# Folding half of batch 1's first DFT stage in a fused global filter and ReGLU FFN kernel

## The chip, the core and the metric

The kernel runs on one core of a Trainium2 chip. Its engines are TensorE (PE in the profile; its weight loads are PEld), VectorE (DVE), ScalarE (ACT), GpSimd (POOL) and SyncE (SP, which only issues DMAs here). The metric is the device time of one execution in microseconds (us). The kernel before was timed three times: 866.41, 866.97 and 868.27 us, median 866.97 us.

## The reference

```
def _attn_ref(x, filt_r, filt_i):            # x: (8, 3008, 256) float32
    X = np.fft.rfft(x, axis=1)
    Y = X * (filt_r + 1j * filt_i)[None, :, :]
    y = np.fft.irfft(Y, n=x.shape[1], axis=1)
    return y.astype(np.float32)

def _moe_ref(x, w_gate, w_val, w_out):       # x: (24064, 256); w: 256x1536, 256x1536, 1536x256
    gate = np.maximum(x @ w_gate, 0.0)
    val = x @ w_val
    return (gate * val @ w_out).astype(np.float32)
```

The second function takes the first one's output with batch and sequence flattened to 24064 tokens.

## The kernel before

**The DFT.** A sequence of 3008 is cut as 94 x 32 (n1, n2). Stage A is a real DFT of length 94 over n1, as a matrix product. Its result is turned so that n2 lies along the partitions, and stage B, the helper `fwd(b, i)`, does the length 32 part for one of six groups of frequencies. `product` multiplies by the filter, `add` joins the products, `inv` goes back along the 32, `load_d` fetches the result turned, and `item_c(k, h)` does the way back along the 94 for one block of 512 tokens, giving `yT`, the input of the FFN.

**Stage A in three forms.** Batch 0: `a_0` with the matrix `WA` (float32), an ACT copy into `AS0`, and a VectorE transpose in four quarters (`turn_0`). Batch 1, all in the prologue: sixteen items of `a_1`, each a 128x512 float32 product in two instructions. Items of the first half of d are copied to `AS1[0]` (a part of `dCb`) and go to DRAM and back (`store_half`, `load_half`); items of the second half go to two `asb` tiles and are transposed on VectorE (`turn_1`, one of four before the FFN, three at its steps 1, 7 and 12). Batches 2 to 7: `load_chunk` brings x in folded order, row n1 beside its mirrored row, `fold_chunk` makes sums and differences on GpSimd (six instructions per chunk, four chunks per batch), and `tiled_a` does 32 small matmuls into four PSUM banks, four copies (two ACT, two VectorE) into an `asb` tile and four stores to `Abuf`; later `load_at_tiled` reads `Abuf` back as `at`, with n2 along the partitions. Each of these stores and reads goes by the SP queue.

**The FFN.** 47 blocks of 512 tokens, twelve steps each. A step is `gv`: two matmuls for the value and two for the gate (128x512 each), an ACT copy `vsb`, and one VectorE instruction `prod` that does the relu and the product. Behind it `o_part` adds four 128x256 output matmuls for the block before; in block 0 there is no block before, so steps 0 to 11 have none. Everything else is hung on steps by a table written out by hand: `at_step(s, f)` calls f after `gv` and `o_part` of step s. All engines work in the order in which the code is written.

**Batch 1's due times.** `end` is 51 for batch 1 and its first two groups start at `end - 37`:

```
        end = (b * S // W - 1) * NFT + C_AT[0] - 5
        starts, gap = ((-37, -25, -13), 4) if b == 1 else ((-43, -30, -17), 5)
```

So `fwd(1, 0)` and `fwd(1, 1)` stand at step 14. They read all of batch 1's `at`.

**Banks.** The eight PSUM banks are handed out in the order in which the code frees them (`free.pop(0)`, `free.append`). A taker waits on the chip until the former owner's last reader is done.

**The prologue's order.** Stage A of batch 0, then `first_b`: for batch 0 `fwd`, products on VectorE and, for three of the twelve (i, e), on GpSimd by way of an ACT copy `xs`, and three inverse blocks `inv(0, q)`, with single items of batch 1 between them (`item(n)`). Then `turn_d` transposes batch 0's result on VectorE in two halves, seven items run beside it, `item_c(0, .)` makes the first `yT`, three more items, and the FFN starts. `warm(n)` issues n matmuls on constant data whose results nobody reads.

Of the kernel before, what the change touches and what calls it, by code (L numbers as in the profile page):

```python
# [116 lines left out]
def kernel(  # L117
# [44 lines left out]
    Abuf = [dram.tile([NROW * N2, D if b > 1 else D // 2], BF16, name=f"Abuf{b}") if b else None for b in range(B)]  # L162
# [9 lines left out]
    AS1 = [dCb[:, 32:48, :].rearrange("p n d -> p (n d)").rearrange("p (l c d) -> p l c d", l=NC2, d=D // 2)]  # L172
# [21 lines left out]
    WHOLE = ((0, 0, NX2 * D), (1, 0, NX2 * D))  # L194
# [3 lines left out]
    conj32 = pro.tile([128, 2], FP32, tag="conj32", bufs=1)  # L198
# [21 lines left out]
    def place_own():  # L220

        o = own.rearrange("p (k r g n) -> p k r g n", k=2, r=2, g=2)
        for i, t in enumerate((I2t, I2u)):
            nc.gpsimd.tensor_copy(t[96:, :, NG // 2 - 2:, :], o[:, i])
# [34 lines left out]

    def a_bank(n2, nn, d0, nd):  # L260

        psA = bank("psA", nn, nd)
        xf = XF[n2 // NX2].rearrange("p (n d) -> p n d", d=D)
        n = n2 % NX2
        nc.tensor.matmul(psA, WA, xf[:, n:n + nn, d0:d0 + nd], start=True, stop=True)  # L265
        return psA

    def a_0(n2, nn, d0, nd):

        psA = a_bank(n2, nn, d0, nd)  # L270
        dq = D // 4
        l, q = n2 % NC2, slice(d0 // dq, (d0 + nd) // dq)
        c = n2 // NC2
        dst = AS0.rearrange("p q (l c) e (g f) -> p l c g q e f", c=2, g=2)[:, l:l + nn, c // 2, c % 2]
        src = psA.rearrange("p n (q e f) -> p n q e f", e=dq // 2, f=2)
        for i in range(nd // dq):
            nc.scalar.copy(dst[:, :, q.start + i], src[:, :, i])
        done(psA)

    def a_1(p, s, h):  # L280

        psA = a_bank(NC2 * p + 4 * s, 4, h * D // 2, D // 2)
        if h and len(AS1) == 1:
            for _ in range(2):
                t = sb.tile([128, NC2 * D], BF16, tag="asb", bufs=3, name="asb")
                AS1.append(t.rearrange("p (l c d) -> p l c d", l=NC2, c=N2 // NC2))
        ts = AS1[1:] if h else AS1[:1]
        w = D // 2 // len(ts)
        for i, t in enumerate(ts):
            nc.scalar.copy(t[:, 4 * s:4 * s + 4, p, :], psA[:, :, i * w:(i + 1) * w])  # L290
        done(psA)

    def turn_a(dst, src):

        nc.vector.transpose(dst.bitcast(FP32).rearrange("p k d -> p d k"),
                            src.bitcast(FP32).rearrange("p n d -> p d n"))
# [6 lines left out]
    def turn_0(q):  # L303
        w = D // 8
        turn_pairs(ats[0][:, :, q * w:q * w + w], AS0[:, q])

    def turn_1(i):
        w = D // 8
        src = AS1[1 + i // 2].rearrange("p l c d -> p (l c) d")
        turn_a(ats[1][:, 1, :, i * w:i * w + w], src[:, :, i % 2 * w:i % 2 * w + w])  # L310

    def new_at(b):
        shape = [2, 32, D // 2] if b else [16, D // 2, 4]
        ats[b] = sb.tile([128, *shape], BF16, tag="at", bufs=1, name="at")

    def turn_d(h):

        e = slice(h * D // 4, h * D // 4 + D // 4)
        turn_pairs(D0[:, :, e], DS0[:, :, e])

    def store_half(b):
        w = N2 * D // 2
        for q in range(4):
            nc.sync.dma_start(_ap(Abuf[b], q * NG * w, [[w, NG], [1, w]]),
                              AS1[0][32 * q:32 * q + NG].rearrange("p l c d -> p (l c d)"))

    def load_half(b):
        w = N2 * D // 2
        for q in range(4):
            nc.sync.dma_start(ats[b][32 * q:32 * q + 32, 0, 0:NG, :],  # L330
                              _ap(Abuf[b], q * NG * w, [[D // 2, 32], [w, NG], [1, D // 2]]))
# [16 lines left out]
    def fold_chunk(b, j):  # L348

        xp = XP[j]  # L350
        t = fs.tile([128, 2, 512], FP32, tag="fold", bufs=1, name="fold")
        tt = nc.gpsimd.tensor_tensor
        tt(t, xp[:, 0:2], xp[:, 2:4], op=ALU.add)  # L353
        tt(xp[:, 2:4], xp[:, 0:2], xp[:, 2:4], op=ALU.subtract)  # L354
        tt(xp[:, 1], xp[:, 2], xp[:, 3], op=ALU.add)
        tt(xp[:, 2], xp[:, 2], xp[:, 3], op=ALU.subtract)
        tt(xp[:, 0], t[:, 0], t[:, 1], op=ALU.add)
        tt(xp[:, 3], t[:, 0], t[:, 1], op=ALU.subtract)
        fold[b, j] = (xp[:, 0], xp[:, 3], xp[:, 1], xp[:, 2])
# [21 lines left out]
    def load_at_tiled(b):  # L381

        ats[b] = sb.tile([128, NG, D], BF16, tag="at", bufs=1, name="at")
        for rr in range(4):
            nc.sync.dma_start(ats[b][32 * rr:32 * rr + 32].rearrange("p j d -> p (j d)"),
                              _ap(Abuf[b], rr * N2 * NG * D, [[NG * D, 32], [1, NG * D]]))

    ON_POOL = ((0, 1), (1, 1), (2, 1))
    ats = {}
# [3 lines left out]
    def fwd(b, i):  # L393

        for e in range(2):
            psXs[b, i, e] = bank("psX", 2, D)
            left[b, i, e] = 2
        for r in range(2):
            for c in range(4):
                for e in range(2):  # L400
                    j = 4 * i + c
                    nc.tensor.matmul(psXs[b, i, e][32 * c:32 * c + 32, r],  # L402
                                     F2[64 * e:64 * e + 64, j, 32 * r:32 * r + 32],
                                     ats[b][64 * e:64 * e + 64, j, :] if b > 1 else
                                     ats[b][64 * e:64 * e + 64, :, j, :] if b else
                                     ats[b][64 * e:64 * e + 64, j // 2, :, j % 2 * 2:j % 2 * 2 + 2],
                                     start=True, stop=True, tile_position=(64 * e, 32 * c))

    def product(b, i, e, k, pool=False):
# [6 lines left out]
        if pool:  # L416
            if not k:
                xs[i] = pro.tile([128, 2, D], FP32, tag="xs", bufs=3, name="xs")
                nc.scalar.copy(xs[i], psX)
            nc.gpsimd.tensor_tensor(p, xs[i], filt, op=ALU.mult)  # L420
        else:
            nc.vector.tensor_tensor(p, psX, filt, op=ALU.mult)  # L422
# [12 lines left out]
    def inv(b, q):  # L435

        psD = [bank("psD", 2, D) for c in range(4)]
        last = 0 if b else 1
        for m in range(2):
# [10 lines left out]
        dst = sb.tile([128, 8, D], BF16, tag="dsb", bufs=3, name="dsb") if b else DS0  # L450
        def out(cs):
            for c in cs:
                copy = nc.vector.tensor_copy if (c % 2 if b else (q, c) in ((1, 3), (2, 0), (2, 1))) else nc.scalar.copy
                if b:
                    copy(dst[:, c:8:4, :], psD[c])
                else:
                    k, g = 4 * q + c // 2, c % 2 * 2
                    copy(dst[:, k:k + 3:2, :, g:g + 2], psD[c].rearrange("p m (f e) -> p m e f", f=2))
                done(psD[c])
        if not b:  # L460
            return out(range(4))
# [10 lines left out]
    def first_b(item):  # L472

        def products(i, es=(1, 0)):
            for e in es:
                for k in range(2):
                    product(0, i, e, k, pool=(i, e) in ON_POOL)

# [4 lines left out]
        make_back_u()  # L483
        products(2)
        warm(3)
        fwd(0, 3)
        products(3, (1,))
# [9 lines left out]
        place_own()  # L497
        inv(0, 1)
        item(2)
        inv(0, 2)  # L500
# [31 lines left out]
    def item_c(k, h):  # L532
# [10 lines left out]
        if h == 0 or k:  # L543
            nc.scalar.copy(dst, psY)  # L544
        else:
            nc.vector.tensor_copy(dst, psY)
# [88 lines left out]
    new_at(0)  # L635
# [12 lines left out]
    load_x(1, sp, ((0, 0, 2 * q), (0, 2 * q, 4 * q), (1, 0, 2 * q), (1, 2 * q, 4 * q)))  # L648
    items = iter([(p, s, h) for p in range(4) for h in range(2) for s in range(2)])

    def item(n):
        for _ in range(n):
            p, s, h = next(items)
            a_1(p, s, h)
            if (p, s, h) == (3, 1, 0):
                new_at(1)
                store_half(1)
                load_half(1)

    first_b(item)  # L660
    load_vg(0, DFF // 2)
    load_vg(DFF // 2, DFF)
    load_o()
    nc.gpsimd.tensor_copy(M1, tabs[:, 578:].rearrange("p (l n) -> p l n", l=2))
    for h in range(2):
        turn_d(h)
    item(7)
    for hh in range(2):
        item_c(0, hh)
    item(3)  # L670
    turn_1(0)
    nc.gpsimd.tensor_scalar(Fti, Fti, conj[:, 0:1], 1.0, op0=ALU.mult, op1=ALU.mult)
    nc.sync.dma_start(WF, nc.inline_tensor(fold_h, name="dft_fold").ap())
# [9 lines left out]
    for k in range(1, 4):  # L683
        at_step((1, 7, 12)[k - 1], lambda k=k: turn_1(k))
    for b in range(1, B):
        end = (b * S // W - 1) * NFT + C_AT[0] - 5
        starts, gap = ((-37, -25, -13), 4) if b == 1 else ((-43, -30, -17), 5)
        if b > 1:
# [3 lines left out]
            for j, e in enumerate((-73, -68, -63, -59)):  # L692
# [6 lines left out]
                at_step(folds[j], lambda b=b, j=j: fold_chunk(b, j))  # L699
# [62 lines left out]
```

## Time and profile before

| | |
|---|---|
| profiled execution, its own time | 865.68 us |
| its span, first to last instruction | 863.8 us |
| median of the three runs | 866.97 us |
| PE busy | 848.7 us, 98% of the span |
| DVE, ACT, POOL busy | 67%, 57%, 53% |
| prologue, to the first FFN matmul | 45.59 us |
| `fwd(1, 0)` starts | 60.44 us |

The profile shows one execution. A row of the timeline gives start and duration in us, the engine, the line of the kernel, the operation, the tile written and those read, shapes and types, and how many instructions were joined in the row; in brackets stands the idle time before it and who ended it. A row that joins instructions can overlap the next, since matmuls are pipelined; the distance between the starts is what counts. Landing times of DMAs are read from the updates of their semaphores in the trace.

### The profile page before, as it was taken

To read this page: it belongs to the slowest core of one execution; us is meant where nothing else is said; L and a number is where in the kernel's file an instruction comes from. 1 tells how busy PE (TensorE), PEld (TensorE's weight loads), DVE (VectorE), ACT (ScalarE), POOL (GpSimd) and SP (SyncE) were. 2 spreads that over 40 slices of the span, in tenths; PEclk is the share of its full clock that TensorE was granted. 3 is DMA by queue.
4 is the path that set the end of the run, shared out by engine and by line. 5 is a ranking of instruction groups with operands and counts; after the bars stand their busy time and mean duration, and the time that the engine had idled before them with its cause. 6 is when DMAs were issued, how large, how long until landed. Compare 5 with 4: busy or idle time off the path is not lost.

```text
span 863.8 us, 20396 instructions
## 1 busy us (share of the span) xinstructions
PE 848.7 (98%) x7587; PEld 498.8 (58%) x7704; DVE 577.8 (67%) x863; ACT 494.6 (57%) x904; POOL 458.4 (53%) x496
## 2 busy tenths in 40 slices
PE   9999999999999999999999999999999999999997
PEld 4456655656556555556556655565655656666665
DVE  3878865777657775577765787658865688555553
ACT  5765565555655556555555555555556555555552
POOL 6747890488986765776666756767450023000001
PEclk9999999999999999999999999999999999999999
DMA  9985365334782339633386333762464422611111
GB/s 250 241 164 122 96 158 138 109 113 110 190 183 88 84 87 192 166 98 98 85 208 142 95 103 100 190 151 74 101 130 108 99 58 52 126 43 29 37 35 52
DMA packets 101366, 101.61 MB, mean 118 GB/s; under 512 B 21827, under 2 KB 89955, under 8 KB 99730
## 3 DMA queue, kind: packets, MB, share of 16 engines
q1 hardware_dynamic: 81986, 77.96, 36.1%
q0 software_dynamic: 18928, 21.82, 11.7%
q8 instruction: 61, 1.00, 0.5%
q10 hardware_dynamic: 352, 0.52, 0.2%
q14 instruction: 39, 0.32, 0.1%
HBM read 58.23 MB, written 45.88 MB: 121 GB/s over the span
## 4 chain that ended last, share of the span: by engine, by line
PE 94%; DMA 2%; issue 1%; DVE 1%; ACT 1%; SPq 1%; POOL 0%; DVEq 0%; ACTq 0%
PE psG L555 29%; PE psO L576 28%; PE psV L555 26%; PE psA L265 3%; PE psF L367 3%; PE psY L538 3%; PE psD L445 2%; PE psX L402 1%; DMA XF<-in_x_dram 1%; DMA Abuf<-asb 1%; ACT vsb L558 1%; DVE prod L560 1%; SPq L190 0%; DVE tt L422 0%; DMA out_dram<-osb 0%
## 5 line engine op out<-in xcount | busy, mean ns | idle before, releaser
L560 DVE SCALAR_TENSOR_TENSOR prod<-psG,vsb 128x512 bf16<-128x512 f32 x564 | 389.4, 691 | 235.8 <-ACT vsb L558 231.6
L558 ACT CAST vsb<-psV 128x512 bf16<-128x512 f32 x564 | 332.2, 589 | 225.8 <-PE psV L555 121.1
L576 PE MATMUL psO<-WoT,prod 128*128 128x256 bf16 x2256 | 336.6, 273 | 0.8
L555 PE MATMUL psG<-yT,WgT 128*128 128x512 bf16 x1111 | 331.8, 379 | 5.2
L555 PE MATMUL psV<-yT,WvT 128*128 128x512 bf16 x1030 | 314.9, 380 | 0.1
L576 PEld LDWEIGHTS <-prod 128*128 128x128 bf16 x2256 | 220.6, 98 | 143.4
L555 PEld LDWEIGHTS <-WgT 128*128 128x128 bf16 x1128 | 110.0, 97 | 133.5
L432 POOL TENSOR_TENSOR pp<-tt,uu 128x256 bf16<-128x256 f32 x84 | 60.9, 725 | 170.7 <-DVE uu L422 162.5
L555 PEld LDWEIGHTS <-WvT 128*128 128x128 bf16 x1128 | 100.3, 98 | 37.3 <-issue 25.6
L544 ACT CAST yT<-psY 128x512 bf16<-128x512 f32 x93 | 54.5, 586 | 43.2 <-PE psY L538 42.6
L589 ACT COPY osb<-psO 128x512 f32<-128x512 f32 x92 | 54.1, 588 | 22.1 <-PE psO L576 20.7
L600 POOL DMA_DIRECT2D out_dram<-osb x5 | 2.6, 534 | 119.6 <-ACT osb L589 118.0
L422 DVE TENSOR_TENSOR tt<-psX,Ftr 128x512 f32<-128x512 f32 (+1 forms) x93 | 63.5, 683 | 0.5 <-PE psX L402 0.5
L422 DVE TENSOR_TENSOR uu<-psX,Fti 128x512 f32<-128x512 f32 (+1 forms) x93 | 63.3, 681 | 0.3 <-DMA Fti<-in_filt_i_dram 0.3
L433 POOL TENSOR_TENSOR pp<-tt,uu 128x256 bf16<-128x256 f32 x84 | 60.9, 726 | 0.0
L353 POOL TENSOR_TENSOR fold<-XF 128x1024 f32<-128x1024 f32 x24 | 56.3, 2347 | 5.8 <-DMA XF<-in_x_dram 5.4
L354 POOL TENSOR_TENSOR XF<-XF 128x1024 f32<-128x1024 f32 x24 | 56.4, 2350 | 1.9
L257 POOL CAST scr<-prod 128x8 f32<-128x8 bf16 x19 | 3.6, 190 | 85.8 <-DVE prod L560 71.7
L340 POOL DMA_DIRECT2D XF<-in_x_dram x76 | 45.6, 602 | 2.0 <-issue 1.3
L374 ACT CAST asb<-psF 128x512 bf16<-128x512 f32 x48 | 25.8, 589 | 34.5 <-PE psF L367 34.5
L374 DVE CAST asb<-psF 128x512 bf16<-128x512 f32 x48 | 30.9, 686 | 18.0 <-PE psF L367 18.0
L538 PE MATMUL psY<-M,dCb 96*128 96x94 bf16 (+19 forms) x604 | 37.9, 200 | 0.0
(71 smaller groups left out, 457.8 us busy)
## 6 DMA issues: line engine op xcount, KB each, us to landing
Dbuf<-dsb SPq DMA_DIRECT2D x84, 128.0 KB
dCb<-Dbuf SPq DMA_DIRECT2D x56, 192.0 KB
XF<-in_x_dram POOLq DMA_DIRECT2D x38, 256.0 KB, 6.7
Abuf<-asb SPq DMA_DIRECT2D x96, 96.0 KB
at<-Abuf SPq DMA_DIRECT2D x24, 384.0 KB
XF<-in_x_dram SPq DMA_DIRECT2D x31, 256.0 KB
XF<-in_x_dram POOLq DMA_DIRECT2D x76, 96.0 KB, 5.1
out_dram<-osb SPq DMA_DIRECT2D x69, 94.0 KB
```

The source lines that it names most:

```text
L353: tt(t, xp[:, 0:2], xp[:, 2:4], op=ALU.add)
L354: tt(xp[:, 2:4], xp[:, 0:2], xp[:, 2:4], op=ALU.subtract)
L374: copy(asf[:, :, q, :], banks[q])
L422: nc.vector.tensor_tensor(p, psX, filt, op=ALU.mult)
L432: nc.gpsimd.tensor_tensor(p[:, 0], tt[:, 0], uu[:, 1], op=ALU.subtract)
L433: nc.gpsimd.tensor_tensor(p[:, 1], tt[:, 1], uu[:, 0], op=ALU.add)
L538: nc.tensor.matmul(psY[:, o:o + w], d_rows(b, n2, h), M1[:, 1, n1:n1 + w] if b == 0 else M1[:NROW, 0, n1:n1 + w], start=True, stop=True)
L544: nc.scalar.copy(dst, psY)
L555: nc.tensor.matmul(pt[:, :W], w[:, h, ft * 128:(ft + 1) * 128], yt[:, h, :], start=(h == 0), stop=(h == 1))
L558: nc.scalar.copy(vsb, psV[:, :W])
L560: nc.vector.scalar_tensor_tensor(prod, in0=psG[:, :W], scalar=0.0, in1=vsb, op0=ALU.max, op1=ALU.mult)
L576: nc.tensor.matmul(psO[:, t % 2], prods[ft][:, t * 128:(t + 1) * 128], WoT[:, ft, :], start=(ft == 0), stop=(ft == NFT - 1))
```

## The change

Batch 1's `a_1` items now cover half of n2 only (eight items instead of sixteen, both halves of d at once) and go to DRAM by `store_a1`; they are read back into half of the partitions of `at` at step 1 of the FFN. The other half of n2 is brought in folded order, as chunks 2 and 3 (`load_chunk(1, 2)`, `load_chunk(1, 3)` on SP): chunk 2 is folded on GpSimd before the FFN, chunk 3 on VectorE in eight instructions at steps 0 to 5, 7 and 8. `tiled_a(1, 2)` stands at step 6, `tiled_a(1, 3)` at step 9, and the read of their half of `at` at step 11. `turn_1`, `store_half` and `load_half` are gone. `fwd(1, 0)` stays at step 14.

In batch 0 the product uu of (3, 1) goes from VectorE to GpSimd; the first half of the value and gate weights is loaded earlier on the GpSimd queue; `place_own` and the copy of `M1` go from GpSimd to ACT; the third inverse block is done in two parts with one item between them, and its copies are split by halves of d, each half followed by its `turn_d`. Behind it stand three items and `warm(10)`, and `warm(2)` behind `item_c(0, .)`; the copies of the first `yT` are shared between ACT and VectorE. The last copy and the last transpose of `a_0` and `turn_0` are split in two. The multiplication of `Fti` by the sign vector moves behind the fold of chunk 2 on GpSimd.

```diff
+    AS1 = dCb[:, 32:48, :]
+    def load_x1(p0, np_):
+        for m in range(3):
+            rows = min(32, N1 - 32 * m)
+            nc.sync.dma_start(XF[0][m:m + 4 * rows - 3:4, 4 * p0 * D:4 * (p0 + np_) * D],
+                              _ap(x, ((N1 + 32 * m) * N2 + NC2 * p0) * D,
+                                  [[N2 * D, rows], [NC2 * D, np_], [1, 4 * D]]))
...
+    def a_1(p, j):
+        psA = a_bank(4 * p + 2 * j, 2, 0, D)
+        nc.scalar.copy(AS1[:, 8 * j + p:8 * j + p + 5:4, :], psA)
         done(psA)
...
+    def store_a1():
+        for rr in range(4):
+            nc.sync.dma_start(_ap(Abuf[1], rr * N2 * NG * D, [[D, NG], [NG * D, 16], [1, D]]),
+                              AS1[32 * rr:32 * rr + NG])
...
-    def fold_chunk(b, j):
+    def fold_chunk(b, j, eng=None, cols=1):
...
+        for i in range(cols):
+            e = slice(i * 2 // cols, (i + 1) * 2 // cols)
+            tt(t[:, e], xp[:, e], xp[:, e.start + 2:e.stop + 2], op=ALU.add)
+            if cols > 1:
+                yield
+            tt(xp[:, e.start + 2:e.stop + 2], xp[:, e], xp[:, e.start + 2:e.stop + 2], op=ALU.subtract)
+            if cols > 1:
+                yield
...
-    def load_at_tiled(b):
+    def load_at_tiled(b, o=0, n=N2):
...
-            nc.sync.dma_start(ats[b][32 * rr:32 * rr + 32].rearrange("p j d -> p (j d)"),
-                              _ap(Abuf[b], rr * N2 * NG * D, [[NG * D, 32], [1, NG * D]]))
+            nc.sync.dma_start(ats[b][32 * rr + o:32 * rr + o + n].rearrange("p j d -> p (j d)"),
+                              _ap(Abuf[b], (rr * N2 + o) * NG * D, [[NG * D, n], [1, NG * D]]))
-    ON_POOL = ((0, 1), (1, 1), (2, 1))
+    ON_POOL = {(0, 1): (0, 1), (1, 1): (0, 1), (2, 1): (0, 1), (3, 1): (1,)}
...
         make_back_u()
+        load_vg(0, DFF // 2)
         products(2)
         warm(3)
         fwd(0, 3)
+        place_own()
+        nc.scalar.copy(M1, tabs[:, 578:].rearrange("p (l n) -> p l n", l=2))
...
-        place_own()
         inv(0, 1)
-        item(2)
-        inv(0, 2)
+        psD = [bank("psD", 2, D) for c in range(4)]
+        inv_part(0, 2, psD, (0,))
+        item(1)
+        inv_part(0, 2, psD, (1,))
+        inv_out(0, 2, psD)
...
-    load_x(1, sp, ((0, 0, 2 * q), (0, 2 * q, 4 * q), (1, 0, 2 * q), (1, 2 * q, 4 * q)))
-    items = iter([(p, s, h) for p in range(4) for h in range(2) for s in range(2)])
+    for p, n in ((0, 1), (1, 1), (2, 2)):
+        load_x1(p, n)
+    for j in (2, 3):
+        load_chunk(1, j, nc.sync)
+    nc.sync.dma_start(WF, nc.inline_tensor(fold_h, name="dft_fold").ap())
+    items = iter([(p, j) for p in range(4) for j in range(2)])
...
-    for h in range(2):
-        turn_d(h)
-    item(7)
+    for _ in fold_chunk(1, 2):
+        pass
+    nc.gpsimd.tensor_scalar(Fti, Fti, conj32[:, 0:1], 1.0, op0=ALU.mult, op1=ALU.mult)
+    item(3)
+    store_a1()
+    warm(10)
     for hh in range(2):
         item_c(0, hh)
-    item(3)
-    turn_1(0)
+    warm(2)
...
-    for k in range(1, 4):
-        at_step((1, 7, 12)[k - 1], lambda k=k: turn_1(k))
+    rest = fold_chunk(1, 3, nc.vector, 2)
+    for s in (0, 1, 2, 3, 4, 5, 7, 8):
+        at_step(s, lambda: next(rest))
+    at_step(8, lambda: next(rest, None))
+    at_step(1, lambda: load_at_tiled(1, 0, 16))
+    at_step(6, lambda: tiled_a(1, 2))
+    at_step(9, lambda: tiled_a(1, 3))
+    at_step(11, lambda: load_at_tiled(1, 16, 16))
```

## The prediction

> **What bounds the kernel now.** The profile's first part and its chain of waits (share of the span by engine) come first:
>
> ```profile
> PE 848.7 (98%) x7587; PEld 498.8 (58%) x7704; DVE 577.8 (67%) x863; ACT 494.6 (57%) x904; POOL 458.4 (53%) x496
> PE 94%; DMA 2%; issue 1%; DVE 1%; ACT 1%; SPq 1%; POOL 0%; DVEq 0%; ACTq 0%
> ```
>
> PE sets the end, and the FFN behind the prologue runs in a fixed order, so a shift of PE near the start reaches the end whole. The reader should therefore ask of each part: does PE start the FFN earlier, get more to do, or wait? Next, PE's timeline around the start of the FFN:
>
> ```profile
> 36.27 6.28 PE L265 MATMUL psA<-XF,WA 128*128 128x512 f32 x14
> 42.41 0.67 PE L538 MATMUL psY<-M,dCb 128*128 128x94 bf16 x12
> 42.93 2.82 PE L265 MATMUL psA<-XF,WA 128*128 128x512 f32 x6
> 45.59 0.59 PE L555 MATMUL psV<-yT,WvT 128*128 128x512 bf16 x2
> ```
>
> Seven items fill PE until `item_c` (42.41), three more until the FFN (45.59). Fourteen instructions in 6.1 us make one item 0.87 us. VectorE's timeline of the same place, with two later rows of stage A's fold copies:
>
> ```profile
> 37.75 4.60 DVE L300 STREAM_TRANSPOSE dCb<-AS 128x2048 f32<-128x2048 f32 x2
> ...
> 51.46 1.50 DVE L560 SCALAR_TENSOR_TENSOR prod<-psG,vsb 128x512 bf16<-128x512 f32 x2 [0.30 <-ACT vsb L558]
> ...
> 130.00 1.29 DVE L374 CAST asb<-psF 128x512 bf16<-128x512 f32 x2 [0.72 <-PE psF L367]
> ```
>
> `turn_d` ends at 42.35 and `item_c` follows at 42.41: the seven items are only cover. SP's timeline shows batch 1's round trip through DRAM and, much later, batch 2's:
>
> ```profile
> 44.68 2.79 SPq L324 DMA_DIRECT2D Abuf<-dCb  x4
> 47.68 3.59 SPq L330 DMA_DIRECT2D at<-Abuf  x4
> ...
> 137.73 1.77 SPq L378 DMA_DIRECT2D Abuf<-asb  x4
> 142.13 1.74 SPq L385 DMA_DIRECT2D at<-Abuf  x4
> ```
>
> Before, the first batch's trip is early: reads issued from 47.68 to 50.96 land by 55.24 (semaphore updates), 5 us before `fwd(1, 0)` at 60.44. Last, a `tiled_a` on PE, and the granted clock at the end of the kernel (third column from the right):
>
> ```profile
> 112.32 0.60 PE L576 MATMUL psO<-WoT,prod 128*128 128x256 bf16 x4
> 112.85 1.14 PE L367 MATMUL psF<-XF,WF 24*32 24x512 f32 x32
> 113.93 0.61 PE L555 MATMUL psV<-yT,WvT 128*128 128x512 bf16 x2
> ...
> 858.00:861.80 3.80, 0.21 (x2) 0.00 (x0) 0.29 (x1) 0.27 (x1) 1.09 (x3) 1.00 0.55 151
> 861.90:863.80 1.90, 0.00 (x0) 0.00 (x0) 0.00 (x0) 0.00 (x0) 0.00 (x0) 0.50 0.01 4
> ```
>
> **Part 1, the start of the FFN: -2.9 us.** VectorE works off 18 products back to back at 0.60 us, the last ending at 33.93; without uu of (3, 1) it ends at 33.33. GpSimd's products start 1.12 apart from 23.70; four end at 28.2, the two weight loads put in front of the rest take 1.54 (0.80 + 0.74), and three more end at 33.1. So the second inverse block ends near 33.45, as before. The first part of the third takes 0.5. The item behind it needs the bank of the first copy of `inv(0, 1)`, free at 34.2; it ends at 35.05, the second part at 35.6. ACT then still has a copy of `inv(0, 1)` and one of the item, and makes its half copies (0.3 to 0.4 each) by 36.75; VectorE's two are beside it. `turn_d` takes 4.6 (37.75 row) and ends at 41.45, `item_c` about 0.7, the split yT copies about 0.4 in place of 0.6 to 0.7: the FFN starts at 42.65 instead of 45.59. Three items (2.6) and `warm(10)` (10 x 0.22) fill PE meanwhile. Bounds: -2.0, if GpSimd's part slips by 0.9, to -3.3, if the item finds a free bank at once. Costed at nothing: the eight items that go (7.0 us of PE), since the end of `turn_d`, not PE, sets `item_c`; `place_own` and M1 on ACT (0.34 to 0.40 each on GpSimd) and the fourth xs (0.56), about 1.7 in a hole of 1.48 on ACT before 27.93, at most 0.3 late, and the second inverse block waits for GpSimd longer than that; the halved last copy and transpose of batch 0, since the second product waits for the Fti load until 23.55 anyway; three smaller first loads, for the same GpSimd.
>
> SP now issues 9 + 12 + 1 loads instead of 12, about 0.63 apart: until 34 instead of 29, with nothing behind them before `store_a1` near 39. GpSimd issues the remaining weights (3.2) until 36.3, folds chunk 2 by the fold rows (2 x 2.35 + 4 x 1.27 = 9.8) until 46 to 48, then Fti (2.8); step 6 comes at 49, so 1 to 3 us remain. `store_a1` and its reads at step 1 have 15 us, against 10.6 that the trip took before.
>
> **Part 2, two tiled_a on PE: +2.3 us.** From the psO start at 112.32 to the next psV start is 1.61, without psF 0.44: 1.17 each.
>
> **Part 3, VectorE's fold: +2.5 us.** Let the FFN start at 0. Steps 0 to 11 last 0.865 each, later ones 1.30, a yT item 0.27; before, 12 x 0.865 + 3 x 1.30 + 2 x 0.27 = 14.85, just the 60.44 - 45.59 of `fwd(1, 0)`. VectorE's first prod can start at 1.25 (psV 59.04, prod 60.29). Until the eighth fold instruction it has 9 prods at 0.61, 8 folds at 0.60 (the filter products of 128x512 float32 are the nearest row, but read PSUM) and two psF copies at 0.64: 1.25 + 5.5 + 4.8 + 1.3 = 12.85. Three transposes of 1.08 that stood there are gone from it, four with the one before step 0. PE comes to `tiled_a(1, 3)` at 10 x 0.865 + 0.54 + 1.17 = 10.36 and waits 2.5. Ends: 1.0 with folds at 0.42, 4.0 if they take 0.8 or chunk 3 lands late. For its second price a page helps: the Trainium skill, "GPSIMD Engine Reference", section "Specifications", says that GpSimd's SBUF interfaces are shared with VectorE and that they contend when a VectorE instruction has two SBUF inputs; no row here has such an instruction, and by it the Fti multiplication could add up to its 2.8 us.
>
> **Part 4, the second trip: +5.5 us.** Let T be the start of the second psF on PE. `fwd(1, 0)` is due 1.14 + 2 x 0.865 + 3 x 1.30 = 6.8 us later. All 24 such excursions in the trace end their last copy 2.61 after the psF start. Then four stores in 1.77, landing 2.0 to 2.6 after issue in the quiet case (137.73), 3.6 to 5.4 beside GpSimd's loads; the first read waits for the third store, so it issues at T + 5.9 at best, the last at T + 6.6 or later. Reads: the quiet ones at 142.13 landed 4.4, 6.3, 8.0 and 9.8 after the first issue, 1.8 apart for 384 KB; the new ones have half the bytes, so 0.9 apart and about 6.2 in all, landing at T + 12.1. By the 192 KB reads of before, 4.3 after issue, it is T + 10.9. Beside batch 2's chunks, whose loads on the GpSimd queue stay at steps 6 and 12, it is T + 15. PE thus waits 4.1 to 8.2; I take 5.5, near the quiet case, since no output stores run before step 17. On PE everything is queued behind this wait: the FFN itself.
>
> **Part 5, the clock: +2.0 us.** The last matmul ends at 858.2, and the granted clock goes to 0.50 at 861.8, 3.6 us later. At the start 18 warm matmuls of 256 columns take 0.21 each, as long as 512 columns take later, until 5.1, 4.0 us after the first. A wait of 5.5 thus costs a restart: 4.0 us at half speed, 2.0 lost; ends 0 and 3.4. By the Trainium skill, "TensorE: Matmul & The Clock Gate", section "What's actually happening", the gate closes after an idle window of about 3.4 us that runs freely; a 5.5 us gap then holds a whole window only about 6 times in 10, and the sum would be 1.2 instead of 2.0, by estimate.
>
> **Sum.** -2.9 + 2.3 + 2.5 + 5.5 + 2.0 = +9.4. Against the profiled execution's 865.7: 875.1. That execution is 1.3 below the median of the runs (866.97), so for runs: 876.4.
>
> **Rivals.** *The trip fits.* If stores and reads are back within 6.8 us of T, no wait and no restart: 866.97 + 1.9 = 868.9, and 867.4 with the lag at its lower end of 1.0. For it: reads of half the size on a queue with little else. Against: copies and store issue alone are 4.4, and no store to `Abuf` landed in under 1.9, no read of `at` in under 4.2. It decides from a trip below about 7 us on; with a lag of up to 2.3 it is then not slower by 0.2%, which is about what a measurement of this kernel can tell from no change.
>
> *The prologue gives more.* With products until 33.3, inverse 0.9, copies 0.6, transposes 4.6 and 1.2 for yT back to back, the FFN would start at 40.6, 5.0 earlier: 9.4 - 2.1 = +7.3, 874.3. For it: VectorE and GpSimd both end their products by then. Against: ACT's five copies between `inv(0, 1)` and `turn_d`. Only with the trip fitting too is it faster, 866.97 + 1.9 - 2.1 = 866.8 with the lag and 864.3 without.
>
> *Loads crowd.* 3.4 MB of x instead of 3.1, in 2 KB pieces, share the DMA engines with the weights, which landed as late as 46.9 before; batch 2's last pieces at 56.3 took 7 to 8 us. If chunk 3 lands after 45, VectorE stands, and everything behind it: +4 or more, 880 to 886.
>
> **How the numbers follow.** Forecast (PE waits at step 14) 0.72, from 871 (-3.3 + 2.3 + 1.0 + 4.1 + 0 on 866.97) to 882; trip fits 0.14, most of it within 0.2%; the longer gain of the prologue 0.05 beside the forecast, 872 to 877, and 0.04 beside a trip that fits, faster; crowded loads 0.05, the upper end. Faster 0.05, same 0.10, slower 0.85. The range 867.5 to 882 leaves out the faster cases, part of the trip that fits and most of the crowded ones.
>
> **What would show it.** Right: the FFN's first psV near 42.7; PE idle about 2.5 us before the second psF and about 5.5 before psX of `fwd(1, 0)`, which ends on a DMA of `at`; a granted clock of 0.5 after it. Wrong: no such wait, the lag hidden, or a PE wait before step 6 for GpSimd's fold or for weights.

## The result, and the profile after

The changed kernel takes 901.43 us (median of 4 runs, 899.35 to 905.89), the kernel before 866.69 us beside it: a ratio of 1.0404, 95% interval 1.0361 to 1.0447. The forecast was 876.4, with a range that ended at 882.0. The sign was right, the size was not. The profiled execution took 899.35 us with a span of 897.6, so 33.7 us more than the profiled one of before.

The page of the changed kernel, first part and chain of waits:

```profile
PE 863.8 (96%) x7764; PEld 500.0 (56%) x7764; DVE 583.4 (65%) x871; ACT 494.4 (55%) x903; POOL 469.4 (52%) x500
PE 84%; DMA 12%; SPq 1%; DVE 1%; issue 1%; POOL 0%; ACT 0%; ACTq 0%; DVEq 0%; POOLq 0%
```

PE was 94% of the chain and is 84%, DMA was 2% and is 12%: the chain now runs through transfers. PE is also busy for 15 us longer, though it has no more work (eight items of 0.87 us less, two `tiled_a` of 1.17 and twelve short `warm` matmuls more). Where this happens stands in PE's timeline, from the FFN's start to the first forward block (in brackets the idle time and who ended it):

```profile
43.56 0.71 PE L570 MATMUL psV<-yT,WvT 128*128 128x512 bf16 x2 [0.23 <-DVE yT L561]
...
53.78 1.01 PE L570 MATMUL psV<-yT,WvT 128*128 128x512 bf16 x2 [5.38 <-DVE prod L575]
...
62.03 2.01 PE L362 MATMUL psF<-XF,WF 24*32 24x512 f32 x4 [3.63 <-DMA Abuf<-dCb]
65.21 2.10 PE L362 MATMUL psF<-XF,WF 24*32 24x512 f32 x28 [1.18 <-DVE prod L575]
...
70.88 2.27 PE L362 MATMUL psF<-XF,WF 24*32 24x512 f32 x32
...
85.60 0.39 PE L398 MATMUL psX<-at,F 64*32 64x256 bf16 x1 [6.71 <-DMA at<-Abuf]
90.88 1.05 PE L398 MATMUL psX<-at,F 64*32 64x256 bf16 x31 [4.88 <-DMA at<-Abuf]
```

The FFN does start earlier (43.56 instead of 45.59). Then PE stands four times before the second excursion, `tiled_a(1, 3)` (5.38, 3.63 and 1.18, and 0.88 not shown: 11.1 us) and twice at `fwd(1, 0)` (11.6 us). The block that ended at 61.1 before ends at 91.9; before, it had no wait:

```profile
60.44 0.63 PE L402 MATMUL psX<-at,F 64*32 64x256 bf16 x32
```

The DMA named at 62.03 is a store that `tiled_a` does not read; VectorE's `prod` of 61.25, which ends at 61.93 and frees a bank, fits better. VectorE's timeline says why PE stood the first time, GpSimd's what was late as well:

```profile
52.43 0.69 DVE L343 TENSOR_TENSOR asb<-XF 128x512 f32<-128x512 f32 x1 [6.78 <-DMA XF<-in_x_dram]
...
53.64 2.23 DVE L346 TENSOR_TENSOR XF<-XF 128x512 f32<-128x512 f32 x1
...
60.21 1.12 DVE L343 TENSOR_TENSOR asb<-XF 128x512 f32<-128x512 f32 x1 [3.73 <-DMA XF<-in_x_dram]
...
61.85 2.71 DVE L346 TENSOR_TENSOR XF<-XF 128x512 f32<-128x512 f32 x1
```

```profile
50.13 2.33 POOL L343 TENSOR_TENSOR asb<-XF 128x1024 f32<-128x1024 f32 x1 [14.03 <-DMA WF<-dft_fold]
52.55 2.78 POOL L346 TENSOR_TENSOR XF<-XF 128x1024 f32<-128x1024 f32 x1
```

Both folds wait for x. The last piece of chunk 2 lands at 49.91, and GpSimd starts its fold 0.2 us later (the profile names the table's load, which landed later; the landing of the chunk fits). The pieces of chunk 3 land from 50.57 to 60.18, and VectorE, whose prods stand behind its fold instructions, stands twice. GpSimd's fold of chunk 2 ends at 60.78 (its last row is not shown), so `tiled_a(1, 2)` would have been late by that alone. SP's timeline shows the loads and both trips through DRAM:

```profile
36.40 8.04 SPq L328 DMA_DIRECT2D XF<-in_x_dram  x2
...
49.98 8.96 SPq L314 DMA_DIRECT2D Abuf<-dCb  x4
61.30 2.82 SPq L381 DMA_DIRECT2D at<-Abuf  x4
...
78.81 1.99 SPq L381 DMA_DIRECT2D at<-Abuf  x4
```

The L328 row shows the mirrored pieces of chunk 3; chunk 2's were issued at 30.65 and 31.33. These four DMAs of 256 KB took 14.5, 18.6, 20.0 and 21.6 us from issue to landing. SP was not done with its loads at 34, as forecast, but after 45; `store_a1` followed at 49.98. The reads of the second trip, issued from 78.81, landed at 83.2, 85.6, 87.9 and 90.7. Last, the granted clock by stretches (third column from the right):

```profile
48.40:65.20 16.80, 5.74 (x13) 1.25 (x11) 9.03 (x9) 2.25 (x4) 13.65 (x7) 0.60 0.59 131
...
78.90:91.86 12.96, 1.37 (x32) 0.66 (x33) 0.77 (x2) 0.00 (x0) 2.32 (x4) 0.63 0.82 130
91.86:96.50 4.64, 4.64 (x24) 2.18 (x17) 1.85 (x4) 1.17 (x2) 1.27 (x2) 0.55 0.00 0
```

The clock was at half from 51.63 to 68.70 and from 82.35 to 96.01, with 9.22 and 5.52 us of PE's work in these stretches. That is 7.4 us of time that full speed would have saved.

Added up on PE: start -2.0, two `tiled_a` +2.3 and 1.1 in them for banks not yet free (the last one takes 2.27, not 1.17), waits 11.1 and 11.6, half clock 7.4: 31.5, of 32.9 us by which PE's output matmuls behind the block trail the same ones of before. The other 1.4 us are not assigned. About 1.9 us more build up behind 240 us, most of it in waits of 0.9 and 0.6 us for the `at` of two later batches (at 402 and 614), and what follows the last output matmul is 1.0 us shorter. That makes the 33.7, up to rounding.

### The profile page after: what moved, and what is told of

It is laid out like the page before. It is cut to its first block, busy times and chain, and to the rows that moved or that the text cites. A ratio compares the mean times of both kernels' runs of the same rounds, so it can differ in the third digit from the quotient of the medians.

```text
span 897.6 us, 20689 instructions
## 1 busy us (share of the span) xinstructions
PE 863.8 (96%) x7764; PEld 500.0 (56%) x7764; DVE 583.4 (65%) x871; ACT 494.4 (55%) x903; POOL 469.4 (52%) x500
## 4 chain that ended last, share of the span: by engine, by line
PE 84%; DMA 12%; SPq 1%; DVE 1%; issue 1%; POOL 0%; ACT 0%; ACTq 0%; DVEq 0%; POOLq 0%
PE psV L570 26%; PE psO L591 25%; PE psG L570 25%; DMA XF<-in_x_dram 4%; DMA at<-Abuf 4%; PE psF L362 3%; PE psY L552 3%; DMA Abuf<-asb 2%; PE psX L398 1%; PE psD L445 1%; DMA out_dram<-osb 1%; DMA Ftr<-in_filt_r_dram 1%; DMA Fti<-in_filt_i_dram 1%; SPq L190 0%; SPq L381 0%
## 5 line engine op out<-in xcount | busy, mean ns | idle before, releaser
L570 PE MATMUL psV<-yT,WvT 128*128 128x512 bf16 x1128 | 338.2, 381 | 6.5 <-DVE prod L575 6.3
L570 PE MATMUL psG<-yT,WgT 128*128 128x512 bf16 x1128 | 337.2, 381 | 0.0
L558 ACT CAST yT<-psY 128x512 bf16<-128x512 f32 x92 | 54.0, 587 | 44.9 <-PE psY L552 44.4
L351 POOL TENSOR_TENSOR XF<-XF 128x512 f32<-128x512 f32 x50 | 63.7, 1274 | 3.9
L346 POOL TENSOR_TENSOR XF<-XF 128x1024 f32<-128x1024 f32 x25 | 59.3, 2370 | 2.0
L351 POOL TENSOR_TENSOR XF<-fold 128x512 f32<-128x512 f32 x48 | 59.9, 1269 | 0.0
L369 ACT CAST asb<-psF 128x512 bf16<-128x512 f32 x52 | 27.9, 589 | 41.5 <-PE psF L362 41.5
L369 DVE CAST asb<-psF 128x512 bf16<-128x512 f32 x52 | 33.5, 686 | 19.0 <-PE psF L362 19.0
```

The costliest lines, as they stand in the source:

```text
L346: tt(xp[:, e.start + 2:e.stop + 2], xp[:, e], xp[:, e.start + 2:e.stop + 2], op=ALU.subtract)
L351: tt(o, i0, i1, op=op)
L369: copy(asf[:, :, q, :], banks[q])
L570: nc.tensor.matmul(pt[:, :W], w[:, h, ft * 128:(ft + 1) * 128], yt[:, h, :], start=(h == 0), stop=(h == 1))
```

## The experiments

**Which load is late.** Two runs take one suspect each. In the first the mirrored pieces of batch 1's chunks go by the GpSimd queue:

```diff
         for i in range(2):
-            eng.dma_start(xp[:, 2 * i + 1, :],
+            (nc.gpsimd if b == 1 else eng).dma_start(xp[:, 2 * i + 1, :],
```

> Theory A, few DMA engines: the two mirrored pieces of each of batch 1's chunks go by SP on four DMA engines (their semaphores show 5 updates, those of GpSimd's loads 16), so they land 15 to 22 us after issue, and GpSimd's fold, VectorE's fold and PE wait for them. By the GpSimd queue the same bytes land within about 8 us: chunk 3 complete by 44 instead of 60.2, PE's waits before the second psF fall from 11.1 us in all to 4 or less, and the first stretch at half clock goes; the wait at fwd(1, 0) stays at 8 to 12. Time 880 to 886. Rival B, too many bytes beside the weights, whatever the engines: chunk 3 still after 52, time 893 or more.

In the second the first half of the value and gate weights is loaded where it was before:

```diff
-        load_vg(0, DFF // 2)
         products(2)
...
     first_b(item)
+    load_vg(0, DFF // 2)
     load_vg(DFF // 2, DFF)
```

> The first half of the value and gate weights is loaded again where it was before, behind the products. Theory A: chunk 3's last piece still lands between 57 and 62, time 899 to 906. Rival B, the weights put ahead are what is in the way: it lands 4 us earlier or more, time 890 to 896.

Measured: 900.61 us for the mirrored pieces (ratio to before 1.0377, 1.0288 to 1.0465) and 900.39 us, one run, for the weights. Neither time moved, but both edits brought the chunks in earlier. With the mirrored pieces on the GpSimd queue the chunks landed by 44.9 instead of 60.2, and the waits before the second excursion shrank from 11.1 to 2.2 us; neither theory had expected that together with an unchanged time. With the weights put back, chunk 2 landed by 42.9 instead of 49.9 and chunk 3 by 56.8 instead of 60.2, between the marks of its two theories, and the same waits shrank to 5.6 us; the FFN started 2.3 us later, and PE then waited 17.8 us at `fwd(1, 0)`. So the weights put ahead have a part in the late chunks too.

Whether four engines make the mirrored pieces slow stays open: on the GpSimd queue they also went out 10 to 16 us earlier. In the kernel before, batch 2's pieces of this size took 7.1 and 8.8 us on SP (5 updates) and 7.3 to 9.8 us on the GpSimd queue (16 updates), which speaks for the rival, too many bytes at once. On the other side, from 48 to 60 us in the changed kernel the DMA engines were only 0.31 to 0.62 busy, while the last pieces of chunk 3 were still in flight. PE's timeline with the pieces on the GpSimd queue:

```profile
30.65 3.75 PE L272 MATMUL psA<-XF,WA 128*128 128x512 f32 x4 [3.35 <-DMA XF<-in_x_dram]
...
48.56 0.71 PE L570 MATMUL psV<-yT,WvT 128*128 128x512 bf16 x2 [0.24 <-DVE yT L561]
...
88.33 0.37 PE L398 MATMUL psX<-at,F 64*32 64x256 bf16 x1 [17.40 <-DMA at<-Abuf]
```

An early item now waits for its own x, as the nine loads for these items took 6.2 to 10.9 us to land instead of 2.5 to 4.9, and the FFN starts 5.0 us later than in the changed kernel. The rest went into the waits at `fwd(1, 0)`: 17.40 and another 2.38 us instead of 11.6. The block ends near 92 all the same.

**Without the loads.** Batch 1's chunks 2 and 3 are not loaded at all:

```diff
-    for j in (2, 3):
-        load_chunk(1, j, nc.sync)
```

> Leaves out the loads of batch 1's chunks 2 and 3, so that batch 1's second half is computed from what batch 0 left there. This is the kernel as the forecast saw it, with no load in the way: if the forecast's other terms hold (VectorE's lag 2.5, wait at fwd(1, 0) 5.5, half clock 2.0) 876; if the wait at fwd(1, 0) is as long as in the changed kernel, 11.6, 881 to 884. Below 870 would say that the second trip is short as well and that late loads explain it all.

Beside it, the first two groups of batch 1's forward blocks stand four steps later:

```diff
-        starts, gap = ((-37, -25, -13), 4) if b == 1 else ((-43, -30, -17), 5)
+        starts, gap = ((-33, -23, -13), 4) if b == 1 else ((-43, -30, -17), 5)
```

> Batch 1's first two groups start four steps (5.2 us) later, at step 18, the next two at step 28. If the second trip ends by the clock of its own transfers, the wait at fwd(1, 0) falls from 11.6 to about 6.4 and the time by 5 to 6, to 894 to 897. Rival: the trip is late because it shares the DMA engines with batch 2's second chunk, issued at step 12, and that is not changed, so the same numbers; what tells the two apart is whether the reads still take over 10 us from issue to landing.

Measured: 895.58 us without the loads (ratio 1.0319, 1.0238 to 1.0399) and 911.74 us, one run, with the later blocks. In the latter the first block still waited 8.3 us, and its four reads took 13.2 us from the first issue, beside batch 2's second chunk: the rival's mark. The inverse blocks then waited 11.3 us for GpSimd's sums: slack ahead of one wait was paid for behind it. The run without the loads is above what either case of its forecast gave. On PE it shows:

```profile
44.23 0.71 PE L570 MATMUL psV<-yT,WvT 128*128 128x512 bf16 x2 [0.23 <-DVE yT L561]
...
58.49 2.23 PE L362 MATMUL psF<-XF,WF 24*32 24x512 f32 x32 [0.60 <-DVE XF L351]
...
85.13 0.37 PE L398 MATMUL psX<-at,F 64*32 64x256 bf16 x1 [18.67 <-DMA at<-Abuf]
```

Here the second excursion comes 14.3 us behind the FFN's start, 1.4 us behind the forecast's 12.85. But the reads, issued from 68.49 on, are complete only at 87.45, 19 us later, and PE waits 20.7 us in two parts. So there is a second cause behind the first. By the landings of the trace, batch 2's second chunk was in flight with these reads: its six DMAs went out on the GpSimd queue from 65.07 to 68.15, and the last landed at 85.13.

**Crowded reads.** The next two runs move batch 2's first two chunk loads behind the place where PE waits, one with all loads, one without batch 1's chunks:

```diff
-            loads, folds = (((6, 12, 20, 30), (22, 34, 46, 46)) if b == 2 else
+            loads, folds = (((15, 17, 20, 30), (22, 34, 46, 46)) if b == 2 else
```

> Only the steps of batch 2's first two chunk loads on the GpSimd queue move, from steps 6 and 12 to 15 and 17, behind the place where the first forward block waits for the second trip. Theory A (the second trip's reads are long because they share the DMA engines with these chunk loads): the four reads land within 6 to 7.5 us of the first one's issue instead of 11.9, the wait at the first forward block falls from 11.6 us to 6 to 8, the clock's restart there is shorter, and the time falls to 893 to 897. Theory B (reads of 16 rows into 16 partitions are slow by themselves): the reads still take about 12 us and the time stays at 899 to 904.

> The same move of batch 2's loads, with the loads of batch 1's chunks 2 and 3 left out (that part of batch 1's output is computed from stale data). Theory A: what is left is the forecast's own case, so the wait at the first forward block falls from 20.7 us (the run with only the loads left out) to 5 to 7, and the time from 895.6 to 875 to 881. Theory B: the wait stays above 12 us and the time at 888 or more.

Measured: 900.61 us (1.0384, 1.0359 to 1.0408) and 886.17 us (1.0218, 1.0189 to 1.0247). In both the four reads were back 8.6 and 8.7 us after the first one's issue, as against 11.9 in the changed kernel and 19.0 in the run without the loads. PE in the run without batch 1's loads, whose reads were issued from 64.30:

```profile
70.01 0.37 PE L398 MATMUL psX<-at,F 64*32 64x256 bf16 x1 [4.54 <-DMA at<-Abuf]
73.06 1.05 PE L398 MATMUL psX<-at,F 64*32 64x256 bf16 x31 [2.68 <-DMA at<-Abuf]
```

These two waits make 7.2 us (a count of 7.5 below takes in 0.26 us at a later batch's first block). This is the forecast's own case, and its range for the wait was 4.1 to 8.2. The time is still above the 875 to 881 expected. Crowding by batch 2's loads is worth 9.4 us here (895.58 to 886.17), batch 1's chunk loads 14.4 us (900.61 to 886.17, by leaving them out). They do not add up from the changed kernel: taking away one alone gave 5.8 or 0.8 us (the 0.8 is within the noise), both together 15.3, since each wait hides part of the other. With all loads kept, moving batch 2's only shifted the loss: PE was 4 us earlier behind the first block and lost that again, 3 us of it near 123, after GpSimd's fold had waited 6.2 us for the moved chunk.

The other way round, batch 2's two loads were moved ahead, to steps 6 and 8, again without batch 1's loads:

```diff
-            loads, folds = (((6, 12, 20, 30), (22, 34, 46, 46)) if b == 2 else
+            loads, folds = (((6, 8, 20, 30), (22, 34, 46, 46)) if b == 2 else
```

> As the run with batch 1's chunk loads left out and batch 2's two chunk loads moved behind the first forward block (886.2), but the loads are moved ahead instead, to steps 6 and 8 (batch 1's output is wrong by the missing loads). Theory A (any GpSimd chunk load that is in flight with the reads stretches them, and the late place cost about 4 us more behind the forward block, where it runs into batch 2's other loads and the first output stores): reads back within 9 us of their first issue, no VectorE wait near 108, 880 to 883. Rival (the trip stays long in the early place too, as the loads are still landing): reads over 12 us, 889 or more.

Measured: 890.80 us (1.0278, 1.0255 to 1.0302): the rival's time, but not its reason. The reads were short, 8.6 us from the first issue, as theory A said. But the loads were in flight when the stores of the second excursion were issued, and these took 11.0 to 11.6 us to land instead of 1.9 to 2.2. PE waited 15.9 us at `fwd(1, 0)`. So these chunk loads can stretch the trip's stores as well as its reads.

**VectorE and GpSimd.** The 886.17 us run once more, with GpSimd's fold of chunk 2 and its multiplication of `Fti` left out:

```diff
-    for _ in fold_chunk(1, 2):
-        pass
-    nc.gpsimd.tensor_scalar(Fti, Fti, conj32[:, 0:1], 1.0, op0=ALU.mult, op1=ALU.mult)
+    fold[1, 2] = (XP[2][:, 0], XP[2][:, 3], XP[2][:, 1], XP[2][:, 2])
```

> The run before with GpSimd's fold of chunk 2 and its multiplication of Fti left out as well (unfolded data and a wrong sign in batch 1). Theory C (VectorE's fold lags because GpSimd's fold and Fti multiplication contend with it): every fold instruction on VectorE takes 0.6 to 0.7 us, PE's waits before the second excursion, 1.9 us with GpSimd busy, go to under 0.5, and the time is 1.5 to 3 us below the run before. Theory D (VectorE has too much work by itself, as forecast with 2.5 us): the waits stay at 1.5 to 2.5 us and the time within 1 us of the run before.

Measured: 884.58 us (1.0205, 1.0168 to 1.0242), 1.6 less than with GpSimd busy, with overlapping runs. VectorE's longest fold instruction with GpSimd busy, what GpSimd did beside it, and the same VectorE instruction with GpSimd quiet:

```profile
48.06 2.71 DVE L343 TENSOR_TENSOR asb<-XF 128x512 f32<-128x512 f32 x1
```

```profile
46.98 3.25 POOL L676 TENSOR_SCALAR Fti<-Fti,conj 128x3072 bf16<-128x3072 bf16 x1
```

```profile
48.23 0.68 DVE L343 TENSOR_TENSOR asb<-XF 128x512 f32<-128x512 f32 x1
```

With GpSimd quiet all eight fold instructions took 0.68 us; with GpSimd busy the eight together took 2.5 us more. The second excursion came 11.84 us behind the FFN's start instead of 14.38. That is contention, worth 2.5 us on PE. Part of it was lost again at a wait near 109, 3.8 us here and 1.3 with GpSimd busy.

**Part 1 alone.** Two runs without chunk loads, fold, excursions and second trip. In the first the second half of `at` was read from the first half's rows, all eight reads at step 1:

```diff
-                              _ap(Abuf[b], (rr * N2 + o) * NG * D, [[NG * D, n], [1, NG * D]]))
+                              _ap(Abuf[b], rr * N2 * NG * D, [[NG * D, n], [1, NG * D]]))
...
-    rest = fold_chunk(1, 3, nc.vector, 2)
...
-    at_step(6, lambda: tiled_a(1, 2))
-    at_step(9, lambda: tiled_a(1, 3))
-    at_step(11, lambda: load_at_tiled(1, 16, 16))
+    at_step(1, lambda: load_at_tiled(1, 16, 16))
```

> Part 1 alone: batch 1's chunks 2 and 3 are neither loaded, folded nor transformed, and the second half of the forward blocks' input is read from the first half's rows at step 1 (batch 1's output is wrong by that). No second excursion, no second trip. Forecast: the FFN starts 2.9 us earlier and the time is 864.1. By the start seen in the run without the chunk loads (44.23 instead of 45.59): 1.4 us earlier, 865.6. If the earlier start is given back behind it: 867 or more.

In the second, GpSimd sets `at` to zero in place of its fold, and only the first half is read:

```diff
-    for _ in fold_chunk(1, 2):
-        pass
+    ats[1] = sb.tile([128, NG, D], BF16, tag="at", bufs=1, name="at")
+    nc.gpsimd.memset(ats[1], 0.0)
...
-    at_step(11, lambda: load_at_tiled(1, 16, 16))
```

> Part 1 alone once more, without the doubled reads that made PE wait at the first forward block in the first such run: the second half of the forward blocks' input is set to zero by GpSimd in the place of its fold, and only the first half's trip is read (batch 1's output is wrong by that; no chunk loads, no fold, no second excursion, no second trip). If part 1 gives what its first psV shows (43.1 to 43.8 instead of 45.6) and nothing gives it back: no wait at the first forward block and 864.6 to 865.4. If the trip, whose stores start later in the queue beside the weight loads, is late for a block that now comes earlier: a wait there and 866.5 or more.

Measured: 870.21 us (1.0051, 1.0030 to 1.0073) and 863.05 us (0.9958, 0.9942 to 0.9973). The first says nothing of part 1: its doubled reads landed at 64.15, and PE waited 5.9 us at `fwd(1, 0)`. In the second nothing waits there:

```profile
43.42 0.71 PE L570 MATMUL psV<-yT,WvT 128*128 128x512 bf16 x2 [0.24 <-DVE yT L561]
```

The FFN starts 2.2 us earlier, and the time is 2.3 to 5.0 us below before by the interval. The forecast of -2.9 lies inside that interval and is a little high for the start; PE's output matmuls come 2.1 us earlier in the profiled execution, and 1.1 us of that is left at the last one.

**The half clock.** The 886.17 us run with its wait at `fwd(1, 0)` filled by 30 matmuls whose result nobody reads:

```diff
+    def fill(n):
+        psJ = bank("psJ", 512)
+        for i in range(n):
+            nc.tensor.matmul(psJ, WvT[:, 0, 0:128], WvT[:, 0, 0:512], start=True, stop=True)
+        done(psJ)
+
+    at_step(14, lambda: fill(30))
```

> The run with batch 1's chunk loads left out and batch 2's moved later (886.2), with 30 idle matmuls of 512 columns put on PE ahead of the first forward block, 6.6 us in the place of its wait of 7.5. Theory A (the half clock behind the wait costs what PE does in it): no stretch of granted clock 0.5 near 69 to 79, where PE had 6.2 us of work before, and the time falls by about 3 us to 883. Rival (the clock falls anyway or the filled wait costs more than it saves): 886 or more.

Measured: 887.36 us (1.0235, 1.0220 to 1.0251), not less. The stretches behind the wait, first unfilled, then filled:

```profile
73.00:78.93 5.93, 5.87 (x47) 2.76 (x48) 2.31 (x4) 1.17 (x2) 1.37 (x3) 0.50 0.00 0
```

```profile
74.00:81.83 7.83, 7.83 (x56) 4.71 (x50) 7.06 (x12) 4.00 (x7) 5.03 (x9) 1.00 0.10 26
```

The clock stayed full, and PE reached the same later point, the first `item_c` behind the block, 38.37 us behind the FFN's start instead of 41.11: 2.7 us of the 3.1 expected. Then they were lost: waits before inverse blocks came to 2.0 us up to that point instead of 0.4, and the one near 109 to 3.0 instead of 1.3, with a stretch at half clock behind it (109.97 to 113.39) that the unfilled run does not have. In all PE fell from 2.4 us ahead of the unfilled run, by its output matmuls, to 1.9 us behind it. GpSimd's timeline pointed to a reason: its fold of batch 2's first chunk, at step 22, waited for the moved load until 96.8 and ran until 106.8, ahead of the sums. So two more runs. The first puts the folds later, the second leaves out GpSimd's early work as well (the edit is shown above):

```diff
-            loads, folds = (((15, 17, 20, 30), (22, 34, 46, 46)) if b == 2 else
+            loads, folds = (((15, 17, 20, 30), (30, 38, 46, 46)) if b == 2 else
```

> The run with the filled wait (887.4), with GpSimd's folds of batch 2's first two chunks at steps 30 and 38 instead of 22 and 34 (batch 1's chunk loads are still left out). Theory A (the gain of the filled wait, seen on PE until 82, was lost where GpSimd waited for the moved chunk until 96.8 and then folded until 106.8 ahead of the sums that VectorE's buffers and the second inverse block wait for): no VectorE wait near 109, none of 1 us before an inverse block, and 882 to 884. Rival (the half clock costs nothing in the end): 886 or more.

> The run before with GpSimd's fold of chunk 2 and its multiplication of Fti left out as well (batch 1's output is wrong by that too). Theory C (contention with GpSimd costs VectorE's fold 2.5 us, the distance between the second excursions of the two earlier runs, 14.4 and 11.8 us behind the FFN's start): 2 to 3 us below the run before. Theory D (it is hidden or handed back): within 1 us.

Measured: 889.52 us (1.0268, 1.0249 to 1.0287) and 887.83 us (1.0250, 1.0230 to 1.0269). The first has the rival's time, and the second lies between its two theories. Later folds did not bring the gain back: at step 30 the fold stood ahead of the next group's sums. GpSimd and PE in the first of the two:

```profile
102.45 2.37 POOL L343 TENSOR_TENSOR fold<-XF 128x1024 f32<-128x1024 f32 x1
...
112.35 0.72 POOL L427 TENSOR_TENSOR pp<-tt,uu 128x256 bf16<-128x256 f32 x1
```

```profile
113.13 0.37 PE L445 MATMUL psD<-pp,I2t 32*64 32x256 bf16 x1 [3.27 <-POOL pp L427]
```

The fold holds GpSimd for 9.9 us, the sum behind it starts at 112.35, and the inverse block that needs it starts 0.8 later. So what the half clock costs in the end time stays open; on PE's timeline, up to 82 us, it is 2.7 us for one wait. Leaving GpSimd's early work out gained 1.7 us, near the 1.6 of the first pair; both are under the 2.5 seen on PE.

**Nothing left out.** The last two runs put the edits into a whole kernel: mirrored pieces on the GpSimd queue and batch 2's loads at steps 15 and 17; then the filled wait and the later folds on top (all these edits are shown above).

> The changed kernel with both causes eased and nothing left out: the mirrored pieces of batch 1's chunks on the GpSimd queue, so that the chunks land by 41, and batch 2's first two chunk loads at steps 15 and 17. Either alone gave 900.6. Theory A (each alone only hands its time to the other): the wait at the first forward block falls from 19.8 us (mirrored pieces alone) to 6 to 9, and the time to 888 to 893. Rival (some third thing holds the first forward block near 92): 897 or more.

> Nothing left out: the run with the mirrored pieces on the GpSimd queue and batch 2's loads at steps 15 and 17 (892.2), with its 8.8 us wait at the first forward block filled by the 30 matmuls and the folds at steps 30 and 38. Theory A: the half clock from 75 to 85, with 5.5 us of PE's work in it, goes, and the late folds' waits with it: 888 to 890. Rival: 892 or more. Neither theory expects a time below the kernel before.

Measured: 892.20 us (1.0293, 1.0276 to 1.0311) and 895.96 us (1.0338, 1.0315 to 1.0361). The first is 9.2 us better than the changed kernel and as expected. The second has the rival's time: it shows the late folds' waits again, 5.6 us before inverse blocks. PE in the first:

```profile
31.94 3.75 PE L272 MATMUL psA<-XF,WA 128*128 128x512 f32 x4 [5.74 <-DMA XF<-in_x_dram]
...
77.11 0.37 PE L398 MATMUL psX<-at,F 64*32 64x256 bf16 x1 [4.55 <-DMA at<-Abuf]
```

An early item waits 5.74 us for its own x, the FFN starts at 50.44, and the trip still costs 7.3 us at `fwd(1, 0)` (the 8.8 us in the text above takes in two waits of later batches). No version with the second half folded beat the kernel before. With every wait gone the parts would leave about -2.9 + 2.3, by estimate; no run shows it.

## Why the prediction was wrong in size

**Part 1 (-2.9)** held within its bounds: -2.0 in the changed kernel, -2.2 alone, and an end time of -2.3 to -5.0 alone. GpSimd's products ended at 33.0, as worked out.

**Costed at nothing: the step that failed first.** The forecast put SP's 22 DMAs "about 0.63 apart: until 34", let GpSimd's fold start at 36.3, when its own issues end, and left "1 to 3 us" to spare. It priced the issue of the loads and not their landing. The mirrored pieces took 14.5 to 21.6 us, the issue itself went on past 45, and GpSimd's fold began at 50.13. This is the rival called *Loads crowd*, with its own mark: chunk 3 landed after 45. It was given 5 in 100 and 880 to 886, below the 901.43 measured, as it had no price for the trip and the clock behind a late chunk. Leaving these loads out gained 14.4 us where nothing else crowds the trip. Why they land late, by the bytes in flight or by few engines, is not separated; moving either the weights or the mirrored pieces brought them in earlier.

**Part 2 (+2.3)** held for the work, but 1.1 us came on top. Banks that a late VectorE had not freed would explain it; that is argued from the code, not tested.

**Part 3 (+2.5).** In the changed kernel 11.1 us, above its upper end of 4.0, which named a late chunk 3. Without the late loads the second excursion came 14.38 us behind the FFN's start, against 12.85 forecast. The work alone is smaller than forecast (11.84 with GpSimd quiet), and contention of 2.5 us is added. The Trainium skill's "GPSIMD Engine Reference", section "Specifications", names just this contention, between GpSimd and a VectorE instruction with two SBUF inputs. The runs agree: 2.71 us beside GpSimd, 0.68 without. The forecast had it only as a sentence beside the sum, with up to 2.8 us for the multiplication of `Fti`; that is the instruction that ran beside the 2.71.

**Part 4 (+5.5)** was 11.6 us, and 7.2 once batch 2's chunks were out of the way. The forecast knew that case ("Beside batch 2's chunks" it is T + 15) and took the quiet one, "since no output stores run before step 17". The loads that its own sentence names, at steps 6 and 12, were the crowd. They bound the trip even when batch 1's loads were gone: 20.7 us.

**Part 5 (+2.0)** was 7.4 us, as there were two long stretches of waiting instead of one of 5.5 us. The half clock began 3.2 and 3.5 us into them, at 51.63 and 82.35, and went on for 3.5 and 5.1 us behind their last wait; around the same places in the other runs it went on for 2.7 to 7.5 us. Its lengths were 17.07 and 13.65 us, five and four times 3.41, the shortest stretch that any run shows within its span. The window of about 3.4 us in the Trainium skill's "TensorE: Matmul & The Clock Gate", section "What's actually happening", agrees with these lengths. Its use in the forecast, a chance that a 5.5 us gap holds a whole window, did not bear on what happened.

The terms were taken as independent. They are not: a late chunk moves the second trip, the trip then meets other loads, and the long waits add half clock.

## What to carry to other kernels

Price a moved load by its landing beside what is then in flight, never by its issue; an issue row says when the queue is free, not when the data is there. Where a round trip through DRAM sits on the path, list every transfer that is due in its 10 us, on all queues, and take the crowded price unless the list is empty. When one wait is removed and the end does not move, look for a second one behind it, and remove both before giving up the first explanation.

## What the runs showed of the hardware

The mirrored loads on SP post 5 updates on their semaphore, the 24-partition loads 13, and the reads and everything on the GpSimd queue 16. The Trainium skill's "DMA: Bandwidth & Descriptors", section "Why a DMA increments its semaphore by 16 and not by 1", says that on an SP queue only the engines in use post an update of their own, that their number is the largest one up to 16 that divides the slowest dimension of both sides, and that the sequencer writes the rest at once. By it these would be 4, 12 and 16 engines, and the counts agree: one update more than 4 and 12, none more than 16. That fewer engines made the loads late is not shown. What was in flight beside them counted, in one run: the first two mirrored pieces took 14.5 and 18.6 us with half of the value and gate weights issued ahead of them, and 7.1 and 11.5 us in the run with those weights behind.

Four reads of 192 KB took 8.7 us from first issue to last landing in quiet, 11.9 and 19.0 beside chunk loads; stores took 1.9 to 2.2 us in quiet and 11.0 to 11.6 beside them.

A VectorE instruction with two SBUF inputs took 2.71 us beside GpSimd's multiplication of `Fti`, four times its 0.68, and 2.23 beside GpSimd's fold. GpSimd's own went from 2.82 to 3.25 and from 2.35 to 2.78.
